# One new token through two attention blocks: B's output projection accumulated in four columns and stored element by element

## The chip, the cores and the metric

The kernel runs on one core of a Trainium2 chip. The metric is the device time of one execution in microseconds (us): 824.31 us before the change, the median of 3 runs (824.25 to 824.35). The engines are named as in the profile: PE (tensor engine; PEld is its loading of weights), DVE (vector engine), ACT (scalar engine), POOL (GpSimd) and SP (SyncE, which issues most of the transfers).

## The reference

Two attention blocks, A and B, each take one token of 512 values, project it to 32 query heads of 128, attend over a cache, and project the 32 x 128 values back to 512. A sees 16,384 keys per head, B only the last 4,096. Everything is bfloat16. The two rows of 512 stand beside each other in the output of 1 x 1 x 1024.

```python
q = (x @ wq) as 32 heads of 128
scores = einsum("bhqd,bhkd->bhqk", q, k) * Dh ** -0.5   # B: k, v = last 4096 rows
p = softmax(scores)
o = einsum("bhqk,bhkd->bhqd", p, v)
out = concatenate([o_A.reshape(1, 1, 4096) @ wo_A, o_B.reshape(1, 1, 4096) @ wo_B], -1)
```

## The kernel before, in words

The work is cut into 20 units: one of B, 16 of A (two heads each), then three more of B (eight heads each). K and V of a unit come by transfers of 4 to 8 MB, issued by SP. DVE multiplies K by the query (L437), adds the products up by halves (L449) and sums the last eight (L456). PE, ACT and DVE then work out the softmax and the sum over V. A small class (`_Stream`) takes the operations of each engine in the order in which the kernel states them, and works out which semaphore each one must wait for; an engine runs its operations in that order. PE's program is one loop over A's units, and the parts that belong to no loop are run behind the condition that no pass is left.

The end of the kernel is what matters here.

- After the last B unit's V half, SP issues the load of B's wo in five pieces (`wo_pieces`, 16, 8, 4, 3 and 1 of 32 rows; L765), each with a semaphore of its own.
- `permute_o(A)` and `project_out_rows(A, ...)` project A's values to one row of 512 on one partition (L640), ACT copies it to SBUF (L645) and stores it (L646). Then come the last unit's softmax and its two sums over V (L604, L611). The second uses the PSUM bank `OC2`, which DVE reads in L611.
- `permute_o(B)` turns B's values so that they meet the rows of wo as these lie in SBUF (L620 to L632); wo is loaded so that a partition holds 32 successive rows of the 4,096.
- `project_out_columns(B, "wo", wo_pieces)` projects. With wo as the stationary operand, a matmul of L656 gives 128 of the 512 results as one column over 128 partitions. For each piece the loop goes over the four groups of 128 results (c), and within it over the piece's rows (r). Each piece has four columns of its own in `OC2`, 20 in all, and each column is an accumulation group of its own. DVE adds up the five pieces (L665, a reduction from 20 to 4 columns). PE transposes the four columns to four rows of 128 (L669), DVE copies these to SBUF as bf16 (L671), and SP stores them as four runs of 256 bytes (L672).
- SP waits for both stores (L646 and L672), and the program ends.

Of the kernel before, what the change touches and what calls it, by code (L numbers as in the profile page):

```python
# [10 lines left out]
F32 = mybir.dt.float32  # L11
BF16 = mybir.dt.bfloat16
P = 128
ACT = mybir.ActivationFunctionType
ALU = mybir.AluOpType
AX = mybir.AxisListType

HQ, DH = 32, 128
# [209 lines left out]
def kernel(  # L228
# [19 lines left out]
    DN = A_wo.shape[1]  # L248
# [7 lines left out]
    def sb(name, shape, dtype):  # L256
        return pool.tile(shape, dtype, tag=name, name=name)

    def pst(name):
        return psum.tile([P, 512], F32, tag=name, name=name)  # L260
# [6 lines left out]
    identf = sb("identf", [P, P], F32)  # L267
# [10 lines left out]
    p_t = sb("p", [P, 2 * CH], BF16)  # L278
# [2 lines left out]
    pm_t = sb("pm", [P, 2 * CH * 4], BF16)  # L281
    r_t = sb("r", [P, 8], F32)
    osb = sb("osb", [P, 512], F32)
    cols = sb("cols", [P, 4], F32)
    sm = pst("sm")
    oc_t = pst("oc")
    TP = [pst(f"tp{i}") for i in range(2)]
    OC2 = pst("oc2")
# [16 lines left out]
    st = _Stream(tc)  # L305
    V, T_, S, G, L = nc.vector, nc.tensor, nc.scalar, nc.gpsimd, nc.sync
# [339 lines left out]
        st.op("ACT", lambda: S.dma_start(out=out[0, 0:1, 0:DN], in_=row), r=["osb"], w=["outA"], dma="outA")  # L646

    def project_out_columns(s, key, pieces):
        nf, npc = DN // P, len(pieces)
        ps = OC2[:, 0 : npc * nf].rearrange("p (k c) -> p k c", k=npc)  # L650
        r0 = 0
        for k, n in enumerate(pieces):
            def mms(k=k, n=n, r0=r0):
                for c in range(nf):
                    for r in range(r0, r0 + n):
                        x = T_.matmul(  # L656
                            ps[:, k, c : c + 1], lhsT=s.wo_t[:, r, c * P : (c + 1) * P], rhs=s.Op[:, r : r + 1],
                            start=(r == r0), stop=(r == r0 + n - 1),
                        )
                return x  # L660

            st.op("PE", mms, r=["Op" + s.n, f"{key}.{k}"], w=["oc2"])
            r0 += n
        first = st.ops["PE"][-npc]
        st.op("DVE", lambda: V.tensor_reduce(  # L665
            out=cols[:, :], in_=ps.rearrange("p k c -> p c k"), axis=AX.X, op=ALU.add
        ), r=["oc2"], w=["cols"])
        pr = TP[0][0:nf, 0:P]
        st.op("PE", lambda: T_.transpose(pr, cols[:, :], identf[:, :]), r=["cols", "identf"], w=["tp0"])  # L669
        rows = p_t[0:nf, 0:P]  # L670
        st.op("DVE", lambda: V.tensor_copy(rows, pr), r=["tp0"], w=["p.0", "p.1"])  # L671
        st.op("SP", lambda: L.dma_start(out=out[0, 0, DN : 2 * DN].rearrange("(c f) -> c f", c=nf), in_=rows),  # L672
              r=["p.0"], w=["outB"], dma="outB")
        return [first]

    wo_pieces = (16, 8, 4, 3, 1)
# [3 lines left out]
    for s in (B, A):  # L680
        s.x_row = flat(KS[1][0:1, :, :])[:, x0 : x0 + D]
        for a, b in x_pieces:
            st.op("ACT", lambda s=s, a=a, b=b: S.dma_start(out=s.x_row[:, a:b], in_=s.x[0, 0:1, a:b]),
                  w=[f"x{s.n}.{a}"], dma=f"x{s.n}{a}")
# [7 lines left out]
        out=identf[:, :], in_=identf[:, :], compare_op=ALU.not_equal, fill=1.0, base=0,  # L692
# [7 lines left out]
    for s in (B, A):  # L700
# [9 lines left out]
          w=["k10", "k11", *(f"x{n}.{a}" for n in "AB" for a, _ in x_pieces)] + [f"k10.{j}" for j in range(4)], dma="K10")  # L710

    parts = []
    for T, un in enumerate(units):
# [5 lines left out]
        if un.last:  # L719
            W, wk = KS[NT % 2], f"k{NT % 2}"  # L720
            s = A
# [41 lines left out]
    r0 = 0  # L763
    for i, n in enumerate(wo_pieces):
        st.op("SP", lambda r0=r0, n=n: L.dma_start(out=B.wo_t[:, r0 : r0 + n, :], in_=src[:, r0 : r0 + n, :]),  # L765
              r=["v1"], w=[f"wo.{i}"], dma=f"woB{i}")
# [12 lines left out]
    parts.append(st.ops["PE"][-1])  # L779
    mark = permute_o(B)  # L780
    parts += project_out_columns(B, "wo", wo_pieces)
    st.op("SP", lambda: None, r=["outA", "outB"], w=["end"])
    with tc.tile_critical(no_gpsimd_drain=True):
# [31 lines left out]
```

## Time and profile before

| what | value |
|---|---|
| median of 3 runs | 824.31 us |
| profiled execution | 824.25 us |
| its span, first to last instruction | 822.47 us (the page rounds to 822.5) |
| DVE busy | 750.4 us, 91% |
| PE busy | 197.9 us, 24% |
| bytes moved | 352.44 MB, mean 429 GB/s |
| mean granted clock of PE | 0.591 |

All times in what follows are in us from the start of the span, unless they are lengths. A line such as L656 is a line of the kernel before. A row of the chain or the timeline gives the start, the length and what ran; in the timeline, brackets at the end give the idle time before and what ended it. "issue" is time in which the engine waited for nothing that the profile shows. The tile that is called `oc2` in the code is shown as `oc` in the profile, since buffer numbers are left out.

### The profile page before, as it was taken

What the parts mean: (1) busy time and instruction counts of PE and PEld (TensorE: products, weight loads), DVE (VectorE), ACT (ScalarE), POOL (GpSimd) and SP (SyncE); (2) the same over time, 40 slices, a digit from 0 to 9 for tenths busy, and PEclk for the clock granted to TensorE, in tenths of its full rate; (3) what the DMA queues carried; (4) which work ended last, traced back from release to release, by engine and by line L of the source; (5) the groups of instructions that cost most, each with busy time, mean ns of one, the idle gap of its engine ahead of it and who ended that gap; (6) DMA issues with size and microseconds to landing.
All of it is one profiled execution on the core that took longest, in us unless ns stands there. A gap on an engine that the chain in (4) does not pass through costs nothing. (4 is left out here: it accounts for less than half of the span.)

```text
span 822.5 us, 5105 instructions
## 1 busy us (share of the span) xinstructions
PE 197.9 (24%) x1985; PEld 99.0 (12%) x1985; DVE 750.4 (91%) x258; ACT 60.0 (7%) x168; POOL 0.7 (0%) x6
## 2 busy tenths in 40 slices
PE   3401212203030303030303212030303030303176
PEld 1100101101010101010101101010101010101035
DVE  2999899999999999999999999999999999999960
ACT  0101000001010100000000001010100000010111
POOL 0000000000000000000000000000000000000000
PEclk9765656565565655565655565555656555655575
DMA  9999999999999999999999999999999999999997
GB/s 383 433 433 433 457 412 450 418 447 421 444 424 441 427 437 430 437 430 437 430 437 430 437 430 437 430 437 430 437 430 437 430 422 445 422 433 431 432 432 298
DMA packets 8094, 352.44 MB, mean 429 GB/s; under 512 B 915, under 2 KB 1046, under 8 KB 1302
## 3 DMA queue, kind: packets, MB, share of 16 engines
q1 hardware_dynamic: 8072, 352.33, 99.2%
q8 instruction: 6, 0.10, 0.0%
q14 instruction: 2, 0.02, 0.0%
q10 hardware_dynamic: 14, 0.00, 0.0%
HBM read 352.32 MB, written 0.00 MB: 428 GB/s over the span
## 5 line engine op out<-in xcount | busy, mean ns | idle before, releaser
L449 DVE TENSOR_TENSOR k<-k 128x16384 bf16<-128x16384 bf16 (+3 forms) x84 | 333.3, 3968 | 2.2
L437 DVE TENSOR_TENSOR k<-k,qA 128x16384 bf16<-128x16384 bf16 x32 | 277.8, 8682 | 21.2 <-DVEq L122 21.1
L564 PE MATMUL oA<-v,pm 128*8 128x512 bf16 x1024 | 89.4, 525 | 111.0 <-PEq L122 111.0
L437 DVE TENSOR_TENSOR k<-k,qB 128x16384 bf16<-128x16384 bf16 x8 | 69.4, 8679 | 1.0 <-DVEq L122 1.0
L471 PE MATMUL sm<-identf,m 128*1 128x128 f32 x24 | 8.1, 369 | 207.8 <-PEq L122 207.8
L493 PE MATMUL sm<-one_f,Mr 1*128 1x1 f32 x48 | 12.4, 335 | 188.8 <-PEq L122 188.8
L564 PEld LDWEIGHTS oA<-v,pm 128*8 128x8 bf16 x1024 | 30.1, 110 | 163.7 <-issue 155.3
L456 DVE TENSOR_REDUCE sc<-k 128x256 f32<-128x2048 bf16 (+1 forms) x21 | 45.9, 2185 | 0.7
L493 PEld LDWEIGHTS sm<-one_f,Mr 1*128 1x128 f32 x48 | 11.2, 300 | 195.1 <-issue 195.1
L512 ACT ACTIVATE bias<-sm 128x1 f32<-128x1 f32 (+1 forms) x20 | 3.4, 171 | 412.0 <-ACTq L122 412.0
L471 PEld LDWEIGHTS sm<-identf,m 128*1 128x1 f32 x24 | 1.7, 80 | 209.7 <-issue 209.7
L576 ACT ACTIVATE osb<-oA,r 128x512 f32<-128x512 f32 x16 | 11.0, 687 | 214.1 <-ACTq L122 214.1
L564 PE MATMUL oB<-v,pm 128*16 128x512 bf16 x192 | 17.6, 546 | 23.1 <-PEq L122 23.1
L586 PE MATMUL oc<-selA,osb 128*128 128x2 f32 x128 | 16.4, 250 | 15.6 <-PEq L122 15.6
L586 PEld LDWEIGHTS oc<-selA,osb 128*128 128x128 f32 x128 | 15.5, 191 | 23.2 <-issue 23.2
L544 PE MATMUL sm<-cs,rowsA 128*128 128x1 f32 x32 | 8.9, 348 | 32.3 <-PEq L122 32.3
L502 ACT ACTIVATE pm<-p,maskA 128x256 bf16<-128x256 bf16 x32 | 14.5, 500 | 0.5
L544 PEld LDWEIGHTS sm<-cs,rowsA 128*128 128x128 f32 x32 | 8.0, 311 | 33.2 <-issue 33.2
L419 PE MATMUL tp<-v,osb 128*128 128x512 bf16 x32 | 9.1, 454 | 10.6 <-DMA v<-in_A_wq_dram 10.6
L516 ACT ACTIVATE p<-sc,bias 128x256 bf16<-128x256 f32 (+1 forms) x24 | 11.3, 470 | 0.6
L488 DVE TENSOR_REDUCE M<-sm 1x2 f32<-1x128 f32 (+1 forms) x20 | 6.0, 298 | 5.8 <-DVEq L122 5.8
L465 DVE TENSOR_REDUCE m<-sc 128x1 f32<-128x256 f32 (+1 forms) x20 | 8.4, 420 | 2.8
(73 smaller groups left out, 108.0 us busy)
## 6 DMA issues: line engine op xcount, KB each, us to landing
k<-in_B_k_cache_dram SPq DMA_DIRECT2D x8, 4096.0 KB, 35.9
v<-in_B_v_cache_dram SPq DMA_DIRECT2D x7, 4096.0 KB, 29.3
v<-in_B_wq_dram SPq DMA_DIRECT2D x1, 4096.0 KB, 12.2
v<-in_A_wq_dram SPq DMA_DIRECT2D x1, 4096.0 KB, 30.5
k<-in_A_wo_dram SPq DMA_DIRECT2D x1, 4096.0 KB, 33.5
k<-in_B_v_cache_dram SPq DMA_DIRECT2D x1, 4096.0 KB, 42.9
v<-in_B_wo_dram SPq DMA_DIRECT2D x1, 2048.0 KB, 25.1
v<-in_B_wo_dram SPq DMA_DIRECT2D x1, 1024.0 KB, 27.0
```

What stands on the lines that cost most here:

```text
L419: x = T_.matmul(out_ap, lhsT=s.xb[:, j, c, :], rhs=wq[:, c, j, g : g + 4, :], start=(k == 0), stop=(k == n - 1),)
L437: return V.tensor_tensor(out=k, in0=k, in1=s.q[:, bass.ds(i, 1), :].broadcast_to([P, CH, DH]), op=ALU.mult)
L449: st.op("DVE", lambda it=None, w=w: V.tensor_tensor(out=k[:, :, 0:w], in0=k[:, :, 0:w], in1=k[:, :, w : 2 * w], op=ALU.add), r=keys, w=keys)
L456: st.op("DVE", lambda it=None: V.tensor_reduce(out=sc[:, l0:l1], in_=un.K[:, l0:l1, 0:8], axis=AX.X, op=ALU.add), r=[f"k{un.k}{u}" for u i ...
L471: i = T_.transpose(sm[0:1, v * P : (v + 1) * P], m_t[:, v : v + 1], identf[:, :])
L493: i = T_.matmul(sm[:, 256 + v : 257 + v], lhsT=Mr[:, v * P : (v + 1) * P], rhs=one_f[:, :], start=True, stop=True,)
L502: return S.activation(out=out, in_=in_, func=ACT.Copy, scale=mask)
L516: st.op("ACT", lambda it=None, v=v: S.activation(out=p_t[:, v * n : (v + 1) * n], in_=sc[:, v * n : (v + 1) * n], func=ACT.Exp, scale=inv, ...
L544: i = T_.matmul(sm[v * w : (v + 1) * w, 264:265], lhsT=s.rows[:, :, :, :].rearrange("p r a b -> p (r a b)"), rhs=cs[:, v : v + 1], start=T ...
L564: x = T_.matmul(s.o[r0 : r0 + un.rows, :], lhsT=un.pm[:, l, :, :].rearrange("p a b -> p (a b)"), rhs=VS[:, 4 * l : 4 * l + 4, :], start=(i ...
L576: st.op("ACT", lambda it=None: S.activation(out=osb[:, :], in_=s.o[:, :], func=ACT.Copy, scale=r_t[:, 0:1]), r=["o" + s.n, "r"], w=["osb"] ...
L586: x = T_.matmul(oc_t[:, 0:w], lhsT=osb[:, j * P : (j + 1) * P], rhs=sel[:, j, :], start=(j == 0), stop=(j == 3),)
```

## The change

The results of all five pieces add up in the same four columns of the PSUM bank. Only the very first matmul of the projection carries the start flag, and only the very last the stop flag. DVE copies the four columns to a bf16 tile of 128 partitions x 4. SP stores that tile straight from its 128 partitions: element (f, c) goes to place 128 c + f of B's half of the output, so each of the 512 elements of 2 bytes has a target of its own. The reduction over pieces, the transpose and the copy of its rows are gone.

```diff
-    cols = sb("cols", [P, 4], F32)
+    cols = sb("cols", [P, DN // P], BF16)
...
     def project_out_columns(s, key, pieces):
-        nf, npc = DN // P, len(pieces)
-        ps = OC2[:, 0 : npc * nf].rearrange("p (k c) -> p k c", k=npc)
+        nf = DN // P
+        ps = OC2[:, 0:nf]
         r0 = 0
         for k, n in enumerate(pieces):
-            def mms(k=k, n=n, r0=r0):
+            def mms(r0=r0, n=n):
                 for c in range(nf):
                     for r in range(r0, r0 + n):
                         x = T_.matmul(
-                            ps[:, k, c : c + 1], lhsT=s.wo_t[:, r, c * P : (c + 1) * P], rhs=s.Op[:, r : r + 1],
-                            start=(r == r0), stop=(r == r0 + n - 1),
+                            ps[:, c : c + 1], lhsT=s.wo_t[:, r, c * P : (c + 1) * P], rhs=s.Op[:, r : r + 1],
+                            start=(r == 0 and c == 0), stop=(r == HQ - 1 and c == nf - 1),
                         )
                 return x
...
-        st.op("DVE", lambda: V.tensor_reduce(
-            out=cols[:, :], in_=ps.rearrange("p k c -> p c k"), axis=AX.X, op=ALU.add
-        ), r=["oc2"], w=["cols"])
-        pr = TP[0][0:nf, 0:P]
-        st.op("PE", lambda: T_.transpose(pr, cols[:, :], identf[:, :]), r=["cols", "identf"], w=["tp0"])
-        rows = p_t[0:nf, 0:P]
-        st.op("DVE", lambda: V.tensor_copy(rows, pr), r=["tp0"], w=["p.0", "p.1"])
-        st.op("SP", lambda: L.dma_start(out=out[0, 0, DN : 2 * DN].rearrange("(c f) -> c f", c=nf), in_=rows),
-              r=["p.0"], w=["outB"], dma="outB")
+        st.op("DVE", lambda: V.tensor_copy(cols[:, :], ps), r=["oc2"], w=["cols"])
+        st.op("SP", lambda: L.dma_start(out=out[0, 0, DN : 2 * DN].rearrange("(c f) -> f c", c=nf), in_=cols[:, :]),
+              r=["cols"], w=["outB"], dma="outB")
```

More of the change, by code (lines that the diff above doesn't have):

```diff
@@ L663, in project_out_columns @@
             r0 += n
-        first = st.ops["PE"][-npc]
-        st.op("DVE", lambda: V.tensor_reduce(
-            out=cols[:, :], in_=ps.rearrange("p k c -> p c k"), axis=AX.X, op=ALU.add
-        ), r=["oc2"], w=["cols"])
-        pr = TP[0][0:nf, 0:P]
-        st.op("PE", lambda: T_.transpose(pr, cols[:, :], identf[:, :]), r=["cols", "identf"], w=["tp0"])
-        rows = p_t[0:nf, 0:P]
-        st.op("DVE", lambda: V.tensor_copy(rows, pr), r=["tp0"], w=["p.0", "p.1"])
-        st.op("SP", lambda: L.dma_start(out=out[0, 0, DN : 2 * DN].rearrange("(c f) -> c f", c=nf), in_=rows),
-              r=["p.0"], w=["outB"], dma="outB")
+        first = st.ops["PE"][-len(pieces)]
+        st.op("DVE", lambda: V.tensor_copy(cols[:, :], ps), r=["oc2"], w=["cols"])
+        st.op("SP", lambda: L.dma_start(out=out[0, 0, DN : 2 * DN].rearrange("(c f) -> f c", c=nf), in_=cols[:, :]),
+              r=["cols"], w=["outB"], dma="outB")
         return [first]
```

## The prediction, made before the changed kernel was run

> **What bounds the kernel now.** I read the busy shares and the slices first. The vector engine (DVE) is busy 91% of the span and the transfers fill the DMA engines from beginning to end; only the last slice thins out. So nearly all of the time is set by 352 MB of caches and by DVE's products, and the change touches neither. What it can move is the tail behind the last weights.
>
> ```profile
> span 822.5 us, 5105 instructions
> ...
> DMA  9999999999999999999999999999999999999997
> ...
> q1 hardware_dynamic: 8072, 352.33, 99.2%
> ```
>
> The first row is the span, the second the share of the DMA engines in 40 slices, the third the queue of SP (SyncE) and its share.
>
> Next I read the chain of work that ended last. Its columns are start, length and what ran.
>
> ```profile
> 790.02 28.25 DMA v<-in_B_wo_dram
> 818.27 0.05 issue
> 818.31 0.61 PE oc L656 x16
> 818.92 0.02 issue
> 818.95 0.19 DVE cols L665
> 819.14 0.04 issue
> 819.18 0.39 PE tp L669
> 819.57 0.02 issue
> 819.59 0.28 DVE p L671
> ```
>
> B's output projection waits for the pieces of wo, the last of which land at 818.27 and 818.59 (landing records of the trace). Then four things follow one upon another: the last matmuls, the sum of the pieces, the transpose on the tensor engine (PE), and the copy out of PSUM. Nothing runs beside them: every row from 818.92 on is a step of the end, so a tenth of a us taken out here is a tenth of a us of the whole time.
>
> Then I read the timeline for the store, and for rows that can price the new steps.
>
> ```profile
> 9.81 0.16 DVE L399 CAST xTB<-tp 128x4 bf16<-128x4 f32 x1 [6.35 <-PE tp L392]
> ...
> 819.59 0.28 DVE L671 CAST p<-tp 4x128 bf16<-4x128 f32 x1 [0.47 <-PE tp L669]
> 819.89 0.35 SPq L672 DMA_DIRECT2D out_dram<-p  x1
> ```
>
> L399 is a copy of exactly the new form: four f32 columns of a PSUM bank to four bf16 columns of SBUF. L672 is the store. The DMA view of the us in which the store runs shows its packets:
>
> ```profile
> DMA packets 8, 0.00 MB, mean 1 GB/s; under 512 B 8, under 2 KB 8, under 8 KB 8
> ```
>
> In the trace's packet records these are four data packets of 256 B, on four DMA engines, at 820.67 to 820.72 us, of 15 to 16 ns each, each followed on its engine 12 ns after its own start by a 4-byte packet that raises the semaphore. The four landings are at 821.02 to 821.07. SP waits for them, and the program's end takes from there to 822.47.
>
> The profiled execution took 824.25 us: 822.47 of span and 1.78 around it. That is 0.06 below the median of 824.31. I add my sum to the 824.25.
>
> **What goes.** From the end of the last matmul (818.92) the store is issued at 819.89. After the change DVE still begins at 818.95, but with a copy of four columns in place of the sum over pieces: 0.16 us by L399, so it ends at 819.11. With the 0.02 that lie between L671's end (819.87) and the store now, the store is issued at 819.13. That is **-0.76 us**, all of it on the path. No later work takes the place of the removed steps: PE has nothing left to do after its last matmul, and DVE nothing after the copy.
>
> **What doesn't move.** The 128 matmuls stay in the same order, and each piece waits for the same transfer. They now add into four columns over all pieces and only one of them carries the start flag. The rows of L656 run from 163 to 187 ns, groups' first matmuls and later ones together, so I cost the flag at nothing. The first piece still waits for DVE's read of the same bank at L611 (812.33 to 812.49), which the transpose and permutation of B's O (812.54 to 813.74) hide as before. The matmuls of a piece lie under the landing of the next; if that cover failed, the largest piece is 1.84 us. The columns tile shrinks from 16 to 8 bytes a partition. On SP, nothing but the final wait is queued behind the store.
>
> **What comes, first: the issue.** The store names 128 partitions of four elements, each going to a place of its own in out, so 512 elements in a three-step pattern. No transfer of before has so many pieces. L672 issues four rows in 0.35 us; the loads of A's K (128 rows) take 0.33; those of B (128 rows in a two-step pattern on the DRAM side) 0.53 to 0.64; wo's pieces (128 rows) 0.43 to 0.59. The length follows the pattern's shape more than the number of rows, so I take 0.53, the nearest: **+0.18 us**, with -0.02 and +0.29 as ends. Packets start 0.43 us after the issue's end now; I let them start as much after the new end.
>
> **Second: the elements.** A transfer of 128 rows is spread over all 16 engines (wo's last piece leaves 16 semaphore packets, the store now leaves four). So each engine gets 8 partitions of four elements, 32 writes of 2 bytes in place of one of 256 B. No data packet of 2 bytes is in the trace. Below lie the 4-byte semaphore packets, 9 ns each. Nearest is the 256 B data packet to the same memory, 15 ns. Above it are the 1 KB packets of wo's last piece, which follow each other on an engine every 42 ns. Far above is a full trip of one write: the last data packet starts at 820.72 and its landing is at 821.07, 0.34 us. I take 15 ns, because it is the nearest data write: 32 x 15 = 0.48 less the 0.015 of now, **+0.46 us**. The ends are 32 x 9 = 0.29 (+0.27) and 32 x 42 = 1.34 (+1.33) as long as writes overlap, and 32 x 340 = 10.9 if none did. The last landing behind the last packet I leave at its 0.34.
>
> By the Trainium skill, *DMA: Bandwidth & Descriptors*, section "Why small descriptors are slow (HBM only)", a packet costs some 3 cycles besides its 32-byte beats; for 2 bytes an estimate from it, with the 850 MHz of the same page, is 4 cycles or 4.7 ns, 0.15 us for 32, and the sum would be 823.8 instead of 824.1. Its 11 cycles for 256 B, 12.9 ns, agree with the 12 to 15 ns of the trace.
>
> **Sum:** -0.76 + 0.18 + 0.46 = -0.12, so 824.25 - 0.12 = **824.1 us**. The likeliest case's own range goes from both low ends and no cost per element at all (-0.78: 823.5) to both high ends with overlapping writes (-0.76 + 0.29 + 1.33 = +0.86: 825.1). This is within 0.2% of 824.31 (1.65 us, about what a measurement of this kernel can tell from no change).
>
> **Rivals.**
> - *Short writes wait for each other.* All 512 elements fall into one KB of out, and neighbouring elements of a word come from different partitions, so from different packets and partly different engines. If the memory has to read, merge and write back a word for each of them, and the next write to it waits, the 32 writes of an engine don't stream. Place: between the first packet and the last landing. Price: between the 42 ns at which full packets follow one another and the 340 ns of a lone write; I take the middle in ratio, 120 ns: 32 x 0.12 = 3.84, so -0.76 + 0.18 + 3.82 = +3.24, **827.5 us**, slower. It decides from (1.65 + 0.76 - 0.18) / 32 = 70 ns per element on. For it: every write to DRAM in this trace is 256 B or more, so none shows that short ones stream. Against it: the DMA engines are idle by then (no packet between 818.2 and 820.6), and nothing in the trace waits on a write but this last step.
>   The Trainium skill, same page, section "Specifications", says that below 512 B the engines do a read-modify-write; no run so far shows it, and the 256 B packets at 15 ns don't show a cost of it.
> - *The issue grows with the number of pieces.* If SP's time went with rows, the 0.64 us of a load of 128 would be 5 ns a row, 512 would take 2.56 in place of 0.35, and the time would be 824.25 - 0.76 + 2.21 + 0.46 = **826.2**. By the difference between 0.59 for wo's first piece and 0.35 for the store's four rows it is 1.9 ns, and 824.9. Against it: 128 rows of A's K are issued in 0.33, less than the four rows of the store.
> - *Nothing is paid.* If the elements of a partition travel as one 8-byte packet, there are 8 packets per engine, under 0.1 us, and with an issue of 0.35 the time is 824.25 - 0.76 + 0.06 = **823.55**. For it: source elements lie next to each other. Against it: their targets lie 256 B apart.
> - *The steps don't leave the path,* because PE or the last landing is late anyway: the last piece lands at 818.59 and its matmuls end at 818.92, so a wait could hide only what is before 818.92, and all that goes lies behind it. I give it no chance of its own.
>
> **How the numbers follow.** Forecast 0.57; short writes wait 0.29; the issue grows 0.08 (half of it still within 0.2%); nothing is paid 0.04; a gain beyond 0.2% from something unseen 0.02, since even the whole 0.94 us between the last matmul and the store are less than 1.65. So faster 0.02, within 0.2% 0.57 + 0.04 + 0.04 = 0.65, slower 0.29 + 0.04 = 0.33. The range takes in the lower bound, 823.4, and the slower rivals' prices up to 827.7; some 0.15 above it (writes that hardly overlap) and 0.02 below are left out.
>
> **What would show it.** In the changed profile: one DVE row of 0.16 us between the last matmul and the store, no row of PE after L658, the store issued about 0.2 us after the last matmul's end (right for the first step); its issue row, 0.53 or above 1 (second); 512 packets of 2 bytes in about 0.5 us behind each other, and the last landing 0.35 behind them (third). If the packets spread over 2 us or more, or if the landing comes well after the last packet, the forecast is wrong by the first rival. If the body before 818 us moves at all, something is at work that I have not seen.

## The result: 11.3 us slower

The changed kernel takes 835.59 us (median of 4 runs, 834.96 to 836.22), the kernel before 824.33 (4 runs, 824.25 to 824.36). The ratio is 1.0137, with a 95% interval of 1.0119 to 1.0154. The forecast of 824.1 was wrong, and so was its range up to 827.7. The profiled execution took 835.74 with a span of 833.96, so 11.49 more than the one before.

The end of the chain of the changed kernel is what the prediction wanted to see. The columns are start, length and what ran:

```profile
790.53 27.71 DMA v<-in_B_wo_dram
818.24 0.05 issue
818.29 0.60 PE oc L658 x16
818.88 0.02 issue
818.91 0.16 DVE cols L667
```

Reduction, transpose and row copy are gone, and the copy takes 0.16. From the landing of the last weights to here the two executions run alike: the matmuls of the last two pieces begin at 818.29, before at 818.31. The timeline and the list of DMA issues show the store (the last column of the list is the time from issue to the last landing):

```profile
818.91 0.16 DVE L667 CAST cols<-oc 128x4 bf16<-128x4 f32 x1 [6.46 <-PE oc L658]
819.10 0.41 SPq L668 DMA_DIRECT2D out_dram<-cols  x1
```

```profile
out_dram<-cols SPq DMA_DIRECT2D x1, 1.0 KB, 13.5
```

So the store is issued at 819.10, 0.80 us earlier than before (unrounded), and lands 13.46 us later; before it was 1.17 us. The DMA view of two stretches says where in these 13.46 us the packets are. First 819.5 to 821, then 821 to 832.6:

```profile
DMA packets 528, 0.00 MB, mean 1 GB/s; under 512 B 528, under 2 KB 528, under 8 KB 528
...
q1 hardware_dynamic: 528, 0.00, 17.0%
```

```profile
DMA packets 0, 0.00 MB, mean 0 GB/s; under 512 B 0, under 2 KB 0, under 8 KB 0
```

All 512 packets of 2 bytes and the 16 that raise the semaphore run in the first stretch; by the packet records from 820.04 to 820.41. Then the DMA engines have nothing to do for nine microseconds, until the semaphore rises for the first engine at 829.51, and it rises for the last at 832.56. From there to the end it is 1.40 us, before 1.41. The accounts close: -0.80 for the store's earlier issue, +12.29 from issue to last landing (13.46 - 1.17), together the 11.49 of the spans.

The Trainium skill, *DMA: Bandwidth & Descriptors*, section "Latency and other measured facts", says that the receipt from the target memory dominates a transfer's fixed cost; the trace agrees in kind, for here nearly all of the time lies between the last packet and the receipt, but the 12 us are none that it gives.

### The profile page after: what moved, and what is told of

Same layout as the page of the kernel before. It is cut to its first block, busy times and chain, and to the rows that moved or that the text cites. A ratio compares the mean times of both kernels' runs of the same rounds, so it can differ in the third digit from the quotient of the medians.

```text
span 834.0 us, 5102 instructions
## 1 busy us (share of the span) xinstructions
PE 197.1 (24%) x1984; PEld 98.6 (12%) x1984; DVE 750.0 (90%) x257; ACT 60.0 (7%) x168; POOL 0.7 (0%) x6
## 5 line engine op out<-in xcount | busy, mean ns | idle before, releaser
L516 ACT ACTIVATE p<-sc,bias 128x256 bf16<-128x256 f32 (+1 forms) x24 | 11.3, 470 | 0.6
L564 PEld LDWEIGHTS oB<-v,pm 128*16 128x16 bf16 x192 | 6.3, 118 | 33.1 <-issue 32.0
```

The costliest lines, as they stand in the source:

```text
L516: st.op("ACT", lambda it=None, v=v: S.activation(out=p_t[:, v * n : (v + 1) * n], in_=sc[:, v * n : (v + 1) * n], func=ACT.Exp, scale=inv, ...
L564: x = T_.matmul(s.o[r0 : r0 + un.rows, :], lhsT=un.pm[:, l, :, :].rearrange("p a b -> p (a b)"), rhs=VS[:, 4 * l : 4 * l + 4, :], start=(i ...
```

## The experiments

The theory after this result is that short writes wait for each other. Three forms of it give the same 12.2 us here, because the numbers happen to agree: each engine makes 32 writes, and each 64 bytes of the target take 32 elements.

- *Engine:* an engine waits for each of its own short writes, 32 x 0.38 us.
- *Shared:* one place takes all short writes in turn, 512 x 24 ns.
- *Word:* only writes into the same few bytes wait for each other.

A rival outside the store is that the accumulation in four columns costs the time.

**Each half alone.** The first run has the accumulation and keeps the transpose and the store of four rows.

```diff
 (kernel before)
-        ps = OC2[:, 0 : npc * nf].rearrange("p (k c) -> p k c", k=npc)
+        ps = OC2[:, 0:nf]
...
-                            start=(r == r0), stop=(r == r0 + n - 1),
+                            start=(r == 0 and c == 0), stop=(r == HQ - 1 and c == nf - 1),
...
-        st.op("DVE", lambda: V.tensor_reduce(
-            out=cols[:, :], in_=ps.rearrange("p k c -> p c k"), axis=AX.X, op=ALU.add
-        ), r=["oc2"], w=["cols"])
+        st.op("DVE", lambda: V.tensor_copy(cols[:, :], ps), r=["oc2"], w=["cols"])
```

> Only the accumulation is changed: all pieces add in four columns, DVE copies 4 columns instead of summing 20; transpose, row copy and store of four rows stay as before. If all of the loss sits in the store (my reading of the changed profile, where the 512 packets are through by 820.4 and the landings come at 829.5 to 832.6), this is 0.03 us faster than before (0.16 for 0.19 in DVE), 824.2 to 824.3, with the landing about 1.2 us after the store's issue. If the accumulation into one bank had a price of its own, some of the 11.3 us would show here.

Measured: 824.22 us against 824.44 before, ratio 0.9999 (0.9990 to 1.0008). The store is issued at 819.75 and its last landing is at 820.93, 1.18 us later. The accumulation costs nothing that can be measured.

The second run sums the pieces as before, as bf16, and stores the 512 elements.

```diff
 (kernel before)
+    cols_b = sb("cols_b", [P, 4], BF16)
...
-            out=cols[:, :], in_=ps.rearrange("p k c -> p c k"), axis=AX.X, op=ALU.add
+            out=cols_b[:, :], in_=ps.rearrange("p k c -> p c k"), axis=AX.X, op=ALU.add
...
-      (transpose, row copy, store of four rows)
+        st.op("SP", lambda: L.dma_start(out=out[0, 0, DN : 2 * DN].rearrange("(c f) -> f c", c=nf), in_=cols_b[:, :]),
+              r=["cols"], w=["outB"], dma="outB")
```

> The other half of the change alone: the five pieces keep their own columns and are summed by DVE as before (written as bf16), and the 512 elements are stored singly, without transpose. If the store is the whole cause, 0.03 us more than the changed kernel in DVE, so 835 to 836, with some 12 us from the last packet to the last landing.

Measured: 835.65 us against 824.38, ratio 1.0136 (1.0121 to 1.0152). From the list of DMA issues of this run:

```profile
out_dram<-cols_b SPq DMA_DIRECT2D x1, 1.0 KB, 14.8
```

The whole loss is in the store.

**Fewer writes in all, as many to the same bytes.** The changed kernel, storing one column of four.

```diff
-        ...dma_start(out=out[0, 0, DN : 2 * DN].rearrange("(c f) -> f c", c=nf), in_=cols[:, :]),
+        ...dma_start(out=out[0, 0, DN : DN + P].rearrange("(f o) -> f o", o=1), in_=cols[:, 0:1]),
```

> The changed kernel, but only the first of the four columns is stored: 128 neighbouring elements, 8 per engine, into 256 bytes; the other 384 results are not written. In the changed kernel the last landing comes 12.5 us after the first packet. Three theories. Engine: each engine waits for each of its short writes, 32 x 0.38 us; here 8 x 0.38 = 3.0 us, total near 826.5. Shared: one place takes all short writes one by one, 512 x 24 ns; here 128 x 24 ns = 3.1 us, total near 826.5. Word: only writes into the same few bytes wait for each other; the elements per stretch of memory are as many as before, so the time stays near 12 us, total near 835.5.

Measured: 838.18 us in one run. A quarter of the writes takes no less, 15.0 us from the first packet to the last landing:

```profile
out_dram<-cols SPq DMA_DIRECT2D x1, 0.2 KB, 15.9
```

Engine and shared theory, both at 3 us, fall. The word theory said 12; by 32 writes to 64 bytes its price per further write would be 0.46 us here, so it is not quite a constant.

**Fewer engines.** The kernel before, with its four rows stored to every fourth place.

```diff
-        ...dma_start(out=out[0, 0, DN : 2 * DN].rearrange("(c f) -> c f", c=nf), in_=rows),
+        ...dma_start(out=out[0, 0, DN : 2 * DN].rearrange("(f c) -> c f", c=nf), in_=rows),
```

> The kernel before with its sum and transpose; only the store differs: the four rows of 128 go to every fourth place of B's half, so the 512 results are stored in permuted order as 512 single elements from four partitions, on four engines with 128 writes each. Engine theory (0.38 us per short write on its engine): 128 x 0.38 = 49 us, total near 872. Word theory and shared theory: as many writes into the same kilobyte as in the changed kernel, 12 us, total 836 to 837 (0.8 us above the changed kernel for the transpose).

Measured: 839.90 us in one run, the store's issue at 819.89 and its last landing at 836.71. That is 16.0 us from the first packet. With four times as many writes per engine it takes 1.3 times as long, not four times. The packets themselves now run until 827.44, but on one engine alone: by 822.48 all but 16 of the 512 are out, and three of the four packets that raise the semaphore with them, which leaves the last 16 to the fourth engine. They go out in groups of four between 824.54 and 827.14. Why it is held up, no run shows. Three us more than the word theory gave, but 32 us less than the engine theory.

**Elements apart from each other.** The changed kernel, with the 512 elements in a scratch tensor in DRAM at a chosen distance; B's half of the output is not written.

```diff
+    far = nc.dram_tensor("far", (4, P, 256), BF16, kind="Internal").ap()
...
-        ...dma_start(out=out[0, 0, DN : 2 * DN].rearrange("(c f) -> f c", c=nf), in_=cols[:, :]),
+        ...dma_start(out=far[:, :, 0].rearrange("c f -> f c"), in_=cols[:, :]),
```

> The changed kernel, but the 512 elements go to a scratch tensor in DRAM, 512 bytes apart from each other, instead of B's half of the output, which is not written. 16 engines with 32 writes of 2 bytes each as before. Word theory: no two writes share a word, so they stream like the packets do (0.35 us) and land 0.34 us later; total 823.5 to 824.3. Engine theory and shared theory: the same 12 us as in the changed kernel, total near 835.6.

Measured: 824.27 us in one run. The same 512 packets of 2 bytes on the same 16 engines land within 1.8 us of the issue:

```profile
far<-cols SPq DMA_DIRECT2D x1, 1.0 KB, 1.8
```

Nothing is left of the 12 us. It is not the short write that is slow, and not the number of them, but that they lie close together. The next three runs change only the 256 in the shape of the scratch tensor, to 32, 16 and 4 elements (64, 32 and 8 bytes).

> The changed kernel with the 512 elements in a scratch tensor (B's half of the output is not written), 64 bytes apart instead of 512. The run with 512 bytes took 824.27, with the last landing 1.8 us after the issue; the changed kernel's took 13.5. If the stretch within which short writes wait for each other is 64 bytes or less, this is as fast: about 1.8 us to landing, 824.3. If it is a larger one (128 to 256 bytes, or a bank behind the whole region), several writes share it and the landing comes later: at 0.38 us per write and 256 bytes, 4 writes, about 2.9 us and 825.4; more if the region as a whole is one place.

> As the run before, with 32 bytes between elements. If the stretch is 64 bytes, two writes share one, and at 0.38 us per write (12.2 us for 32 in the changed kernel) the landing comes 0.4 us later than with 64 bytes: about 2.2 us. If it is 32 bytes, nothing changes: 1.8 us and 824.3.

> As the two runs before, with 8 bytes between elements: 512 writes over 4 KB. With a stretch of 64 bytes 8 writes share one, 8 x 0.38 = 3.0 us: landing about 4.5 us after the issue, 827. With 32 bytes 4 writes share one and each would cost 0.76 (12.2 us for 16): the same 3.0 us. If the writes of the whole region go one by one at 24 ns, 12 us and 835.6.

Measured, one run each: 824.01, 824.55 and 826.96 us. The same row of the three profiles, for 64, 32 and 8 bytes:

```profile
far<-cols SPq DMA_DIRECT2D x1, 1.0 KB, 1.8
```

```profile
far<-cols SPq DMA_DIRECT2D x1, 1.0 KB, 2.4
```

```profile
far<-cols SPq DMA_DIRECT2D x1, 1.0 KB, 4.6
```

64 bytes are as good as 512, and 32 are not: the stretch within which writes wait for each other is longer than 32 bytes, and the 64-byte run points to one no longer than 64. All three came close to what a stretch of 64 bytes gave before the runs (1.8, 2.2 and 4.5 us). In records of the trace:

| 512 elements of 2 bytes | writes to 64 bytes | first packet to last landing, us | over the 64-byte run, per further write |
|---|---|---|---|
| 512 bytes apart | 1 | 0.89 | |
| 64 bytes apart | 1 | 0.85 | |
| 32 bytes apart | 2 | 1.47 | 0.61 |
| 8 bytes apart | 8 | 3.70 | 0.41 |
| changed kernel, 2 bytes apart | 32 | 12.52 | 0.38 |

Counted by 64 bytes, the time grows with the number of writes to the same stretch, by some 0.4 us for each. That is about the 0.34 us which a lone write took in the kernel before from its packet to its landing.

A longer stretch with a lower price isn't excluded by the slow rows. With 256 bytes, 128 writes of the changed kernel share a stretch, which makes 0.09 us for each further one. For 32 and 8 bytes this gives 0.6 and 2.9 us above the 64-byte row, measured 0.61 and 2.85; a stretch of 64 bytes with 0.38 gives 0.4 and 2.6. (What was expected of the 64-byte run kept the price of 0.38 for the longer stretch too, and so asked too much of it.) Against 256 bytes speaks the 64-byte run: three further writes per stretch would add up to 0.28 us, and it isn't slower than the run with 512 bytes (0.85 and 0.89, one run each). They would add less if the writes to a stretch went out far enough apart, and the records don't say which write went where. A stretch of 512 bytes or more, at one price per write, is out by the run with one column: it has half the writes to such a stretch and takes no less time. So the stretch is longer than 32 bytes and at most 256, and 64 is the likeliest; the counts below go by 64.

**Longer elements.** A version that stores to the right places: the weights are every fourth column of wo, so that a partition holds four neighbouring results.

```diff
-                            ps[:, c : c + 1], lhsT=s.wo_t[:, r, c * P : (c + 1) * P], rhs=s.Op[:, r : r + 1],
+                            ps[:, c : c + 1], lhsT=s.wo_t[:, r, :].rearrange("p (f c) -> p c f", c=nf)[:, c, :], rhs=s.Op[:, r : r + 1],
...
-        ...dma_start(out=out[0, 0, DN : 2 * DN].rearrange("(c f) -> f c", c=nf), in_=cols[:, :]),
+        ...dma_start(out=out[0, 0, DN : 2 * DN].rearrange("(f c) -> f c", c=nf), in_=cols[:, :]),
```

> The changed kernel with wo's columns taken in steps of four as weights, so that a partition holds four neighbouring results and the store is 128 writes of 8 bytes to the right places. 8 writes share 64 bytes instead of 32. If a write's price doesn't depend on its bytes, 8 x 0.38 = 3.0 us in place of 12.2: total about 826.5, slower than before by 2 us and faster than the changed kernel by 9. If the price went with the bytes of partly written words, it would stay at 835. The stepped weights may cost something in PE; its rows will show it.

Measured: 825.39 us against 824.29, ratio 1.0014 (1.0004 to 1.0024). It recovers 10 of the 11 us and is still slower than before. The last rows of PE and the store:

```profile
818.26 0.69 PE L658 MATMUL oc<-OpB,v 128*128 128x1 bf16 x16 [0.25 <-DMA v<-in_B_wo_dram]
...
818.99 0.16 DVE L667 CAST cols<-oc 128x4 bf16<-128x4 f32 x1 [6.58 <-PE oc L658]
819.18 0.35 SPq L668 DMA_DIRECT2D out_dram<-cols  x1
```

The stepped weights cost 0.1 us in the last 16 matmuls. The list of DMA issues has the landing:

```profile
out_dram<-cols SPq DMA_DIRECT2D x1, 1.0 KB, 2.7
```

From the first packet to the last landing it is 1.90 us, half of the 3.70 that the 8-byte distance took with as many writes per 64 bytes. Two things differ between these runs, the bytes of a write and the number of writes in all; the next run has 128 writes of 2 bytes at the same distance.

```diff
+    far = nc.dram_tensor("far", (P, 4), BF16, kind="Internal").ap()
...
+        ...dma_start(out=far[:, 0:1], in_=cols[:, 0:1]),
```

> One column of 128 elements of 2 bytes, 8 bytes apart, into a scratch tensor of 1 KB (B's half of the output is not written): the same 128 targets as in the run with 128 writes of 8 bytes, whose last landing came 1.7 us after the last packet, against 3.3 us for 512 writes 8 bytes apart, both with 8 writes to 64 bytes. If the price goes with the number of writes to a stretch and in the whole, not with their bytes, this is as the run with 8 bytes: 1.7 us, total near 824.9. If a write of 2 bytes costs more than one of 8, it is near 3.3 us and 826.6.

Measured: 825.36 us in one run:

```profile
far<-cols SPq DMA_DIRECT2D x1, 0.2 KB, 3.0
```

It is 2.22 us from the first packet and 2.02 from the end of the last one. That is nearer to the 8-byte run (1.90 and 1.70) than to the 512 writes (3.70 and 3.32): the bytes of a write, 2 or 8, hardly matter. What is left, that 64 stretches of 8 writes take longer than 16, isn't explained by a fixed price per write and stretch.

**A version from the findings.** Accumulation in four columns, and the transpose in bf16 ahead of the old store.

```diff
 (first experiment, and)
-    cols = sb("cols", [P, 4], F32)
+    cols = sb("cols", [P, 4], BF16)
...
-        pr = TP[0][0:nf, 0:P]
-        st.op("PE", lambda: T_.transpose(pr, cols[:, :], identf[:, :]), r=["cols", "identf"], w=["tp0"])
+        pr = TP[0][0:nf, 0 : P // 2].bitcast(BF16)
+        st.op("PE", lambda: T_.transpose(pr, cols[:, :], ident[:, :]), r=["cols", "ident"], w=["tp0"])
```

> A version made from what the runs showed: accumulation in four columns, the copy to bf16, and a transpose in bf16 (before: f32), with the store of four runs of 256 bytes as before. From rows: DVE 0.16 for 0.19, the transpose near the 0.23 to 0.29 of L620 for 0.37 to 0.39, the row copy at most 0.28. That is 0.1 to 0.2 us less than before, 824.1 to 824.2, which five rounds can hardly tell from no change.

Measured: 824.15 us against 824.38, ratio 0.9997 (0.9988 to 1.0006). The end of its timeline:

```profile
819.13 0.16 DVE L665 CAST cols<-oc 128x4 bf16<-128x4 f32 x1 [6.46 <-PE oc L656]
819.35 0.08 PEld L667 LDWEIGHTS tp<-ident,cols 128*4 128x4 bf16 x1 [0.34 <-DVE cols L665]
819.35 0.27 PE L667 MATMUL tp<-ident,cols 128*4 128x128 bf16 x1 [0.25 <-DVE cols L665]
819.66 0.21 DVE L669 COPY p<-tp 4x128 bf16<-4x128 bf16 x1 [0.36 <-PE tp L667]
819.90 0.35 SPq L670 DMA_DIRECT2D out_dram<-p  x1
```

From DVE's first row to the store it is 0.77 us where it was 0.94, so each step is as short as was expected. The whole time can't be told from that of the kernel before.

## Why the prediction was wrong, point by point

- **What bounds the kernel:** right. The change works only behind 818.9, and from the landing of the last weights to there the two executions agree within 0.04 us (those weights were issued 0.51 us later than before, 790.53 and 790.02, and it made no difference).
- **What goes, -0.76:** right. From the end of the last matmuls to the store's issue it is 0.22 us, before 0.97.
- **The accumulation at nothing:** right; alone it can't be told from no change, and the rows of L658 run from 163 to 187 ns as before.
- **The issue, +0.18:** the size came out, but by luck. The row itself went from 0.35 to 0.41, only +0.06; the first packet, which was to follow the row's end after the same 0.43, follows after 0.53. From issue to first packet it is 0.94 us, before 0.78, so +0.17 in all. The rows of 128 elements take 0.33 to 0.35, those of 512 take 0.39 to 0.41, so the issue does not grow in step with the number of pieces; that rival is out.
- **The elements, +0.46:** this step failed, in its second half. The packets stream even faster than I took: all are through within 0.37 us of the first, which for 32 on an engine is a spacing of some 11 ns. What I "leave at its 0.34", the time from the last packet to the last landing, became 12.16 us. I priced a write by how fast its engine sends it and took the receipt as a constant. The rows that I used, packets of 256 B to DRAM and packets of 1 KB that load wo into SBUF, are none of short writes to DRAM; none could show that such writes meet.
- **The rival of writes that wait** named the wait and its place in time (that the memory reads, merges and writes back is not shown), and its marks came out as stated ("if the landing comes well after the last packet"). Two things in it were wrong. Its price was a middle of 120 ns between 42 and 340, and the measured one is 0.38 us per write, even above the end that gave 10.9 us and that the range left out. And it counted the writes of an engine. The run with elements 512 bytes apart has the same 32 writes per engine and takes 0.89 us; the count that matters is that of the writes which meet in the same few bytes. By 64 bytes it is also 32 in this kernel, by chance.
- **The Trainium skill's read-modify-write** (the Trainium skill, *DMA: Bandwidth & Descriptors*, section "Specifications", below 512 B): as a price per short write it doesn't show, for 512 writes of 2 bytes that lie 64 bytes apart land in 0.85 us. If each of them reads and writes back, it does so in parallel with the others. The rule of the same page of the Trainium skill to keep the last dimension contiguous ("Rules for kernel authors") holds here, for a reason that it doesn't give.

What stays open: what makes the writes wait, and whether in the memory or on the way to it. The runs show that writes which meet wait, bounds of the stretch and a rough price, not the part. Nor is the price constant: by stretches of 64 bytes it is 0.61 us for the second write, 0.38 on average for 31 further ones, 0.46 in the run with one column, about 0.2 with 128 writes 8 bytes apart. Part of that is scatter: the profiled executions of the changed kernel and of its store alone differ by 1.3 us in the same interval (12.52 and 13.82), and the ten runs of the version with 8-byte elements lie between 825.11 and 826.10, with the profiled one the fastest. Whether it matters that writes of several engines meet isn't separated from their number either: in the run with four rows each 64 bytes take writes of all four engines, and for the other runs the records don't say which engine wrote which element.

## What to carry to other kernels

Price a store by its landing, not by its packets: find the last packet and the last landing in the records, and ask for the time between them. Count how many separate writes fall into the same 64 bytes of DRAM; each beyond the first cost some 0.4 us in most of these runs (0.15 to 0.6 in all), so the 0.75 us that sum, transpose and row copy took beyond a plain copy, so that one write takes 256 neighbouring bytes, were cheap. And where a bound of the cost has been worked out and nothing but a guess speaks against it, the range should reach to it.

## What the runs showed of the hardware

Single elements are no trouble by themselves: 512 of them on 16 engines, 64 bytes or more apart, went out in 0.38 us and were confirmed 0.5 us later. A quarter of the elements, packed into 256 bytes, took no less than all of them in a kilobyte (15.0 us in one run against 12.5 and 13.8). And the packets that raise the semaphore stand in the records at 820.41 at the latest, while the semaphore rose 9 to 12 us later: a packet record is no proof that the write has been done.
